# Attention, a top-2 router and eight experts in one kernel: the last group's tail ahead of the first expert, whole-group loads of q and k, and stores from ScalarE's queue

## The chip, the cores and the metric

The kernel runs on one core of a Trainium2 chip. The metric is the device time of one execution in microseconds (us); the time of the kernel before is the median of three runs. The profile is one execution taken with the hardware profiler. Engines are named as in the profile: PE (TensorE matmul) and PEld (its weight load), DVE (VectorE), ACT (ScalarE), POOL (GpSimd), SP (SyncE). L559 is line 559 of the kernel before.

## The reference

Block-causal attention over 8 batches of 8 heads, 576 tokens of 64 elements, and then a mixture of 8 experts over all 4608 tokens; each token goes to two experts.

```python
def _attn_ref(q, k, v):
    scores = scale * np.matmul(q, k.transpose(0, 1, 3, 2))
    mask = block_i >= block_j                      # blocks of 64 positions
    scores = np.where(mask, scores, -1000000000.0)
    attn = softmax(scores)                         # [...] written out with max and sum
    return np.matmul(attn, v)

def _moe_ref(x, w_gate, w_noise, noise, w1, w2):   # x: 4608 x 512, w1: 8 x 512 x 1024, w2: 8 x 1024 x 512
    logits = x @ w_gate
    noise_scale = np.log1p(np.exp(x @ w_noise))
    noisy_logits = logits + noise_scale * noise
    top2 = np.argpartition(-noisy_logits, 2, axis=1)[:, :2]
    # [...] softmax over the two logits gives top2_w
    for e in range(E):
        for k in range(2):
            mask = top2[:, k] == e
            h = np.maximum(x[mask] @ w1[e], 0.0)
            out[mask] += top2_w[mask, k, None] * (h @ w2[e])
    return out
```

## The kernel before

Attention works through four groups (`g`) of two batches, nine tiles of 128 tokens each. A group has 26 slots (`UG`); in each slot a piece of scores is multiplied and exponentiated (`score_unit`), and then everything that was put at that slot runs: transposes of q and k, AV tiles, transposes of x, steps of the router, and loads. AV of a group's second half of heads, its x transposes, its router and its scatters lie in the slots of the next group. The program's order is the order of the code; an engine does its instructions in that order.

```python
def load_qk(g, chunks):
    for ch in chunks:
        for nm, src in (("q", qv), ("k", kv)):
            t = raw_pool.tile([P, 2, 512], BF16, tag="r" + nm)      # raw_pool: bufs=8
            t0 = g * TG + ch
            if ch < 4:
                nc.gpsimd.dma_start(out=t, in_=src[:, t0:t0 + 6:5, :])
            else:
                nc.gpsimd.dma_start(out=t[:, 0, :], in_=src[:, t0, :])
            raws[(g, nm, ch)] = t
```

The router gives each token a row in each of its two experts' tables, and 18 indirect stores a group put the tokens into DRAM (`xd`, one array per half of the tokens). Groups 0 and 1 are half 0, groups 2 and 3 half 1.

```python
def scatter(g, j):
    # [...] one tile of 128 tokens, one of its two experts
    ins = nc.gpsimd.indirect_dma_start(out=xd[half]..., in_=xrs[g][:, idx, :].bitcast(I32), ...)
    tc.add_manual_dep(ins.ins, pace[-1], SYNC_DEP, reason="spreads the descriptors over time")

def load_x(b):                       # the rows of one expert and half, transposed: "row tile"
    half, e = SEQ[b]
    xg = ffn["x"].tile([P, DB, CAP], BF16, tag="xg", name="xg") if b else xa
    ins = nc.sync.dma_start_transpose(out=xg, in_=xd[half][e * CAP:(e + 1) * CAP, 0:Dm])
    # [...] waits for all 36 scatters of the half
```

The experts come in 16 batches (`SEQ`: three experts of half 0, three of half 1, then the halves in turn). A batch has eight steps of layer 1 and five of layer 2; `layer1(b + 1, 0)` stands ahead of `layer2(b, 0)`.

```python
def layer2(b, c):
    yp = av_ps.tile([P, Dm], F32, tag="av")                         # av_ps: bufs=2
    for fb in range(FB):
        nc.tensor.matmul(out=yp, lhsT=hs[b][:, fb, c * P:(c + 1) * P], rhs=w2sb[:, fb, :], ...)
    if e + 1 < E:
        ysb = ffn["y"].tile([P, Dm], BF16, tag="ysb", bufs=4)
        ins = nc.scalar.activation(out=ysb, in_=yp, func=AF.Copy, scale=w)
        pace.append(ins.ins.name)
        nc.sync.dma_start(out=yd[half][e * CAP + c * P:e * CAP + (c + 1) * P, :], in_=ysb)
    if c < LT[e]:
        # yo = yp * w + the gathered row of the token's other expert; scattered to the output by GpSimd

# the last group (g == 3), r0 = 104:
avs, xts_ = (0, 0, 1, 1, 2, 2, 3, 3, 4, 4), range(2, 7)             # slots of AV tiles and x transposes
rsl = (6, 6, 7, 8, 8, 9, 9, 10, 12, 13, 13, 13, 14, 14, 14, 14)     # slots of the 16 router steps
r1 = 14                                                             # slot of the first scatter
# [...]
slot = NG * UG                                                      # 104
for i in range(2):                                                  # slots 104 and 105 stand alone
    run(slot)
    slot += 1
# [...] then one step of the experts, and what was put at the slot, in turn
```

The weighted rows of every expert but the last go to `yd` by a store from SyncE's queue; the row tiles are loaded on the same queue. GpSimd issues all loads of q, k, v and weights, all scatters, gathers and output stores.

Of the kernel before, what the change touches and what calls it, by code (L numbers as in the profile page):

```python
# [19 lines left out]
def kernel(  # L20
# [88 lines left out]
    hq_pool = right.enter_context(tc.tile_pool(name="hq", bufs=1, side="right"))  # L109
    raw_pool = raws_up.enter_context(tc.tile_pool(name="raw", bufs=8, side="right"))  # L110

# [81 lines left out]
    def load_qk(g, chunks):  # L193

        for ch in chunks:
            for nm, src in (("q", qv), ("k", kv)):
                t = raw_pool.tile([P, 2, 512], BF16, tag="r" + nm)
                t0 = g * TG + ch
                if ch < 4:
                    nc.gpsimd.dma_start(out=t, in_=src[:, t0:t0 + 6:5, :])  # L200
                else:
                    nc.gpsimd.dma_start(out=t[:, 0, :], in_=src[:, t0, :])
                raws[(g, nm, ch)] = t

# [25 lines left out]
    def transpose_qk(g, nm, ch):  # L230
        dst = qT if nm == "q" else kT
        tp = tr_ps.tile([P, 1024], BF16, tag="tr")


        if ch in (0, 1, 2, 3):
            raw = raws[(g, nm, ch)]
            p0, p1, c0, nb = 0, P, ch * 1024, 16
        else:
            raw = raws[(g, nm, 4)]
            p0 = 0 if ch == "4A" else 64  # L240
            p1, c0, nb = p0 + 64, 4 * 1024, 8
        n = nb * 64
        if nm == "q":
            to = tp[:, 0:n].rearrange("p (b r j) -> p b r j", b=nb, r=8)
        else:
            to = tp[:, 0:n].rearrange("p (r b j) -> p b r j", b=nb, r=8)
        for r in range(8):
            if nb == 16:
                for hf in range(2):
                    nc.tensor.transpose(to[64 * hf:64 * hf + 64, :, r, :], raw[:, hf, r * 64:(r + 1) * 64], ident)  # L250
            else:
                nc.tensor.transpose(to[p0:p1, :, r, :], raw[p0:p1, 0, r * 64:(r + 1) * 64],  # L252
                                    ident[p0:p1, p0:p1])
        if nm == "q":
            nc.vector.tensor_copy(dst[p0:p1, c0:c0 + n], tp[p0:p1, 0:n])
        else:
            ko = dst[p0:p1, c0:c0 + n].rearrange("p (b j r) -> p b j r", b=nb, j=8)
            ki = tp[p0:p1, 0:n].rearrange("p (r b j) -> p b j r", r=8, b=nb)
            if ch == 1:
                nc.vector.tensor_copy(ko, ki)  # L260
            else:
                nc.scalar.activation(out=ko, in_=ki, func=AF.Copy)  # L262
        if ch == 0:

            nc.vector.tensor_copy(dst[64:128, 72 * 64:73 * 64], dst[64:128, 0:64])
# [104 lines left out]
    def router(g):  # L370
# [37 lines left out]

        c2 = rt.tile([P, TG, E], F32, tag="c2")
        nc.vector.tensor_tensor_scan(out=c2.rearrange("p t e -> p (t e)"),  # L410
# [32 lines left out]
        yield  # L443
        ps = rt.tile([P, E, TG], F32, tag="ps")
        nc.vector.tensor_tensor(out=pos, in0=pos, in1=ms, op=ALU.mult)
        nc.vector.tensor_tensor(out=ps, in0=pos[:, 1], in1=pos[:, 0], op=ALU.subtract)
        yield
        sl2 = rt.tile([P, 2, TG], F32, tag="sl2")
        pk = rt.tile([P, 2, E, TG], F32, tag="pk")
        nc.vector.tensor_tensor(out=pk, in0=oh, in1=ps.unsqueeze(1).to_broadcast([P, 2, E, TG]),  # L450
# [30 lines left out]
    def scatter(g, j):  # L481
        half = g // 2
        idx, i = divmod(j, 2)
        ins = nc.gpsimd.indirect_dma_start(  # L484
            out=xd[half].bitcast(I32), out_offset=bass.IndirectOffsetOnAxis(
                ap=slots[:, g * TG + idx, i:i + 1], axis=0),
            in_=xrs[g][:, idx, :].bitcast(I32), in_offset=None,
            bounds_check=XR - 1, oob_is_err=False)
        tc.add_manual_dep(ins.ins, pace[-1], SYNC_DEP, reason="spreads the descriptors over time")
        key = f"scat{half}"  # L490
        if scat[half]:
            tc.declare_no_dep(ins.ins, group=key, reason="rows of one half are distinct")
        tc.add_to_no_dep_group(key, ins.ins)
        scat[half].append(ins.ins.name)
# [14 lines left out]
    def load_rec(half):  # L509
        rc = rec_pool.tile([P, E, CT, NREC], I32, tag="rc", name="rc")  # L510
        ins = nc.sync.dma_start(out=rc.rearrange("p e c w -> p (e c) w"),
# [6 lines left out]
    def read_rec(half):  # L518
# [3 lines left out]
        def tmp(nm, dt=F32):  # L522
            return rec_pool.tile([P, E, CT], dt, tag=nm, name=nm)


        is0 = tmp("is0")
        nc.vector.tensor_tensor(out=is0, in0=f[0], in1=rowid, op=ALU.is_equal)
        wr = rec_pool.tile([P, E, CT], F32, tag=f"wrow{half}", name="wrow")
        nc.vector.tensor_tensor(out=wr, in0=is0, in1=f[4], op=ALU.mult)
# [6 lines left out]
        nc.vector.tensor_scalar(oth, oth, 0.0, float(XR - 1), op0=ALU.max, op1=ALU.min)  # L536
        orow = rec_pool.tile([P, E, CT], I32, tag=f"orow{half}", name="orow")
        nc.vector.tensor_copy(orow, oth)
# [8 lines left out]
        nc.vector.tensor_tensor(out=mt, in0=mt, in1=fill, op=ALU.mult)  # L547
        tr = rec_pool.tile([P, E, CT], I32, tag=f"trow{half}", name="trow")
        nc.vector.tensor_scalar(tr, mt, -1.0, float(TOKM), op0=ALU.mult, op1=ALU.add)
# [16 lines left out]
    def layer2(b, c):  # L566
# [7 lines left out]
        if e + 1 < E:  # L574
            ysb = ffn["y"].tile([P, Dm], BF16, tag="ysb", bufs=4)
            ins = nc.scalar.activation(out=ysb, in_=yp, func=AF.Copy, scale=w)  # L576
            pace.append(ins.ins.name)
            nc.sync.dma_start(out=yd[half][e * CAP + c * P:e * CAP + (c + 1) * P, :], in_=ysb)
        if c < LT[e]:
# [34 lines left out]
    NB = len(SEQ)  # L614
    rec_pool = keep
    todo = {}
# [47 lines left out]
    def spread_nz(eh, hf):  # L664
# [7 lines left out]
        nc.vector.tensor_copy(dst[:, :, :, 8], src[:, :, :, hf, 8])  # L672

    def flags():
        for i in range(NH):
# [29 lines left out]
    nc.gpsimd.dma_start(out=wgn[:, :, E:2 * E], in_=moe_w_noise.rearrange("(b p) e -> p b e", p=P))  # L705
    load_qk(1, (4, 0, 1))

# [3 lines left out]
    for g in range(NG):  # L711
# [6 lines left out]
        if not last:  # L718
            for nm, ch, i in (("q", 0, 14 if g else 19), ("k", 0, 17 if g else 22), ("q", "4B", 22), ("k", "4B", 21)):
                at(s0 + i, transpose_qk, g + 1, nm, ch)  # L720
            for i, (fn, *a) in enumerate(v_loads(g + 1)):
                at(s0 + 9 + i, fn, *a)
            at(s0 + 13, load_qk, g + 1, (2,))
            at(s0 + 16, load_qk, g + 1, (3,))
        if g + 2 < NG:
            for i, ch in ((20, 4), (22, 0), (24, 1)):
                at(s0 + i, load_qk, g + 2, (ch,))
        for i, a in enumerate((15, 16, 17, 18, 18, 19, 20, 21, 22, 23)):
# [11 lines left out]
        else:  # L740
            avs, xts_ = (0, 0, 1, 1, 2, 2, 3, 3, 4, 4), range(2, 7)
            rsl = (6, 6, 7, 8, 8, 9, 9, 10, 12, 13, 13, 13, 14, 14, 14, 14)
            r1 = 14
# [19 lines left out]
    for k in range(4):  # L763
        at(2 * UG - 6 + k, load_w, wE, 0, k)
        at(2 * UG + 20 + k, load_w, wE, 1, k)
    for u in range(NG * UG):
        score_unit(*divmod(u, UG))
        run(u)
        if u == 3 * UG + 13:
            raws_up.close()  # L770
            ffn["x"] = raws_up.enter_context(tc.tile_pool(name="xgp", bufs=3, side="right", reuse_waits="tile"))
            wM = raws_up.enter_context(tc.tile_pool(name="wM", bufs=1, side="right", reuse_waits="tile"))
            at(3 * UG + 19, load_x, 0)
            at(3 * UG + 20, load_x, 1)
            at(3 * UG + 21, load_rec, 0)
            at(4 * UG, load_x, 2)
            for k in range(4):
                at(3 * UG + 22 + 3 * k, load_w, wM, 2, k)

    slot = NG * UG  # L780
    at(slot + 6, read_rec, 0)
    at(slot + 80, flags)
    at(slot + 90, read_flags)
    steps = []
    for b in range(NB):
# [3 lines left out]
        steps += [(layer2, b, c) for c in range(CT)]  # L789
    for i in range(2):  # L790
        run(slot)
        slot += 1
    WL = {}
    XL = {(2, 3): 3, (3, 1): 4, (3, 5): 5, (4, 2): 6}
    for b in range(5, NB - 2):
        XL[b, 1] = b + 2
    for fn, b, j in steps:
        fn(b, j)
        if fn is layer1:
            if (b, j) == (2, 3):  # L800
                load_rec(1)
            if (b, j) in XL:
                load_x(XL[b, j])
            if (b, j) == (3, 3):
                read_rec(1)
# [9 lines left out]
        slot += 1  # L815
        if slot == NG * UG + 6:
            top.close()
            wL = top.enter_context(tc.tile_pool(name="wL", bufs=2, reuse_waits="tile"))
            ffn["y"] = top.enter_context(tc.tile_pool(name="yp", bufs=4, reuse_waits="tile"))
            ffn["yg"] = [ffn["y"].tile([P, Dm], BF16, name=f"yg{i}", bufs=1) for i in range(GB)]  # L820
            for t in ffn["yg"]:
                nc.vector.memset(t, 0.0)
            for i, pool in enumerate((wL, wL, wE, wE, wM)):
                for k in range(4):
                    WL[3 + 2 * i + k // 2, (2, 6)[k % 2]] = (pool, 3 + i, k)
    assert not todo, sorted(todo)
# [89 lines left out]
```

## Time and profile before

| | |
|---|---|
| time, median of 3 runs | 493.08 us (488.45 to 499.44) |
| span of the profiled execution | 504.7 us |
| PE busy | 409.2 us (81%) |
| ACT busy | 253.2 us (50%) |
| POOL busy | 255.8 us (51%) |
| DVE busy | 161.2 us (32%) |
| layer 1, 960 matmuls of `hp` from `xg` | 137.7 us, 305 ns each |
| layer 2, 640 matmuls of `yp` | 143.8 us, 382 ns each |
| scatters, 72 on GpSimd | 71.2 us, 988 ns each |
| stores of `yd`, 70 on SP's queue | 128 KB each, landing 2.2 us after the issue (median) |
| row tile loads of `xg`, 15 on SP's queue | landing after 9.0 us (median) |
| loads of two tiles of q, 16 on GpSimd | 256 KB each, landing after 8.1 us (median) |

The profile's page gives busy times by engine, the span in 40 slices, the chain of waits that ended last, and groups of instructions by line. A group's line reads: line, engine, operation, output and input tiles, shape, count, busy us and mean ns, and the idle time of the engine just ahead, with what ended it. The attention part ends near 145 us; the experts begin with the first row tile, `xa`.

### The profile page before, as it was taken

Reading aid. Unit: us, or ns where it says so; the run is one execution under the profiler, and the core shown is the slowest. Engines: PE = TensorE matmul, PEld = TensorE weight load, DVE = VectorE, ACT = ScalarE, POOL = GpSimd, SP = SyncE. Lnnn points to the kernel's source line nnn. Section 1 sums busy time; section 2 is a strip of 40 time slices with the busy share of each in tenths; the row PEclk is TensorE's granted clock in tenths of the full one; section 3 lists DMA queues with packets and bytes.
Section 4 is the critical chain, followed back from the end, with each engine's and each line's share of the span. In section 5 each row is a group of like instructions: output and inputs, shape, how many; then the busy total and the mean of one; then the engine's idle time right before and its main releaser. Section 6 shows DMA issues by size and latency. Waiting matters only on the chain.

```text
span 504.7 us, 9922 instructions
## 1 busy us (share of the span) xinstructions
PE 409.2 (81%) x3952; PEld 250.9 (50%) x3952; DVE 161.2 (32%) x508; ACT 253.2 (50%) x343; POOL 255.8 (51%) x309
## 2 busy tenths in 40 slices
PE   2889889889730999919599999999942999999980
PEld 2466656557420746504346655664521565556540
DVE  1677687787840580003000011011100102211220
ACT  2989888878820245513335544554502454455210
POOL 8776674588577456723002234337240546656530
PEclk9989989989875999978989999999985999999995
DMA  8999999899929983462926877997999789994320
GB/s 136 158 147 186 214 185 206 202 126 166 206 107 183 190 192 111 163 102 76 201 75 135 173 169 172 190 165 134 136 104 183 184 178 221 200 202 138 123 79 17
DMA packets 134826, 78.68 MB, mean 156 GB/s; under 512 B 96193, under 2 KB 124611, under 8 KB 134772
## 3 DMA queue, kind: packets, MB, share of 16 engines
q0 software_dynamic: 70560, 55.79, 68.7%
q1 hardware_dynamic: 64212, 22.18, 24.5%
q8 instruction: 33, 0.54, 0.4%
q14 instruction: 21, 0.17, 0.1%
HBM read 68.28 MB, written 33.13 MB: 201 GB/s over the span
## 4 chain that ended last, share of the span: by engine, by line
PE 53%; DMA 17%; issue 9%; DVE 8%; ACT 6%; POOL 5%; SPq 0%; POOLq 0%; DVEq 0%; ACTq 0%
PE yp L571 21%; PE hp L559 18%; DMA yd<-ysb 5%; DMA xg<-xd 4%; ACT esc L295 4%; PE sc L292 3%; PE av L334 3%; PE tp L250 2%; POOL out_dram L583 2%; DMA xa<-xd 2%; DMA yg<-yd,orow 2%; DVE xr L350 2%; DMA xd<-xr,slots 2%; PE av L345 2%; DMA t<-in_q_dram 2%
## 5 line engine op out<-in xcount | busy, mean ns | idle before, releaser
L559 PE MATMUL hp<-xg,w1sb 128*128 128x320 bf16 x960 | 137.7, 305 | 32.6 <-ACT hq L562 16.4
L559 PEld LDWEIGHTS <-w1sb 128*128 128x128 bf16 x1024 | 101.5, 100 | 94.8 <-DMA xa<-xd 18.1
L571 PE MATMUL yp<-w2sb,hq 128*128 128x512 bf16 x640 | 143.8, 382 | 1.2 <-DVE yo L581 1.0
L562 ACT ACTIVATE hq<-hp 128x640 bf16<-128x640 f32 x128 | 90.0, 704 | 105.7 <-PE hp L559 105.6
L581 DVE SCALAR_TENSOR_TENSOR yo<-yp,wrow,yg 128x512 f32<-128x512 f32 x46 | 34.5, 751 | 263.7 <-ACT ysb L576 220.5
L571 PEld LDWEIGHTS <-hq 128*128 128x128 bf16 x640 | 63.0, 98 | 77.0 <-issue 7.2
L295 ACT ACTIVATE esc<-sc 128x1024 bf16<-128x1024 f32 x96 | 94.2, 1026 | 11.5 <-PE sc L292 10.9
L576 ACT ACTIVATE ysb<-yp,wrow 128x512 bf16<-128x512 f32 x70 | 48.1, 687 | 95.1 <-PE yp L571 74.6
L484 POOL DMA_INDIRECT xd<-xr,slots x72 | 71.2, 988 | 47.4 <-issue 12.5
L599 POOL DMA_INDIRECT yg<-yd,orow x46 | 47.6, 1034 | 89.9 <-ACT hq L562 59.7
L583 POOL DMA_INDIRECT out_dram<-yo,trow x46 | 45.8, 995 | 75.4 <-DVE yo L581 62.8
L292 PE MATMUL sc<-hq 64*128 64x512 bf16 (+4 forms) x320 | 40.0, 319 | 11.9 <-ACT esc L295 10.5
L207 POOL DMA_DIRECT2D vt<-in_v_dram x40 | 34.3, 866 | 8.2 <-PE av L345 3.9
L334 PE MATMUL av<-vt,esc 128*128 128x65 bf16 x640 | 32.6, 204 | 5.6 <-DVE xr L350 5.3
L334 PEld LDWEIGHTS <-esc 128*128 128x128 bf16 x640 | 25.7, 104 | 19.3 <-DVE xr L350 11.8
L350 DVE TENSOR_TENSOR xr<-av,rden 128x256 bf16<-128x256 f32 x72 | 30.6, 425 | 2.7
L250 PE MATMUL tp<-ident,t 128*64 128x128 bf16 x512 | 23.1, 239 | 3.4 <-DMA t<-in_q_dram 2.4
L559 PE MATMUL hp<-xa,w1sb 128*128 128x320 bf16 x64 | 10.9, 320 | 18.0 <-DMA xa<-xd 18.0
L262 ACT ACTIVATE hq<-tp 128x1024 bf16<-128x1024 bf16 (+1 forms) x20 | 17.1, 855 | 12.0 <-PE tp L252 6.8
L349 DVE RECIPROCAL rden<-av 128x4 f32<-128x4 f32 x72 | 13.4, 187 | 30.3 <-PE av L334 24.8
L292 PEld LDWEIGHTS <-hq 64*128 64x128 bf16 x320 | 12.6, 96 | 20.2 <-issue 12.6
L250 PEld LDWEIGHTS <-t 128*64 128x64 bf16 x512 | 17.7, 120 | 7.8 <-DMA t<-in_q_dram 2.5
(122 smaller groups left out, 239.2 us busy)
## 6 DMA issues: line engine op xcount, KB each, us to landing
yd<-ysb SPq DMA_DIRECT2D x70, 128.0 KB, 2.2
w1sb<-in_moe_w_dram POOLq DMA_DIRECT2D x16, 512.0 KB, 7.1
w2sb<-in_moe_w_dram POOLq DMA_DIRECT2D x16, 512.0 KB, 6.5
t<-in_q_dram POOLq DMA_DIRECT2D x16, 256.0 KB, 8.1
t<-in_k_dram POOLq DMA_DIRECT2D x16, 256.0 KB, 8.0
vt<-in_v_dram POOLq DMA_DIRECT2D x32, 128.0 KB, 8.4
xd<-zero SPq DMA_DIRECT2D x16, 132.0 KB, 7.3
xd<-xr,slots POOLq DMA_INDIRECT x72, 4.1
```

What stands on the lines that cost most here:

```text
L250: nc.tensor.transpose(to[64 * hf:64 * hf + 64, :, r, :], raw[:, hf, r * 64:(r + 1) * 64], ident)
L292: nc.tensor.matmul(out=sc[:, hf, off:off + z - a], lhsT=kT[sl, c0 + jt * P:c0 + jt * P + P], rhs=qT[sl, c0 + a:c0 + z], start=True, stop=True)
L295: ins = nc.scalar.activation(out=esc[:, hh, :, piece * 512:(piece + 1) * 512], in_=sc, func=AF.Exp, scale=scale)
L334: nc.tensor.matmul(out=av[:, hh, :], lhsT=esc[:, hh, hf, c:c + P], rhs=vb[:, 4 * hf + jt, h, :], start=(jt == 0), stop=(jt == ib))
L350: nc.vector.tensor_tensor(out=xr[:, idx, st * SET * D:(st + 1) * SET * D].rearrange("p (h d) -> p h d", h=SET), in0=av[:, :, 0:D], in1=rde ...
L484: ins = nc.gpsimd.indirect_dma_start(out=xd[half].bitcast(I32), out_offset=bass.IndirectOffsetOnAxis(ap=slots[:, g * TG + idx, i:i + 1], a ...
L559: nc.tensor.matmul(out=hp[:, n, 0:NW], lhsT=w1sb[:, db, fb * P:(fb + 1) * P], rhs=xgs[b][:, db, n * NW:(n + 1) * NW], start=(db == 0), sto ...
L562: ins = nc.scalar.activation(out=hs[b][:, fb, :].rearrange("p (n w) -> p n w", n=2), in_=hp[:, :, 0:NW], func=AF.Relu)
L571: nc.tensor.matmul(out=yp, lhsT=hs[b][:, fb, c * P:(c + 1) * P], rhs=w2sb[:, fb, :], start=(fb == 0), stop=(fb == FB - 1))
L576: ins = nc.scalar.activation(out=ysb, in_=yp, func=AF.Copy, scale=w)
L583: ins = nc.gpsimd.indirect_dma_start(out=out, out_offset=bass.IndirectOffsetOnAxis(ap=trow[half][:, e, c:c + 1], axis=0), in_=yo, in_offse ...
L599: ins = nc.gpsimd.indirect_dma_start(out=yg, out_offset=None, in_=yd[half][0:e * CAP, :], in_offset=bass.IndirectOffsetOnAxis(ap=orows[hal ...
```

## The change

It has several parts. The last group's AV, its transposes and the first three router steps run in seven slots ahead of the first expert step, to lie in the wait for the first row tile. q and k of groups 1 to 3 come in one load each, to spare GpSimd's issues; two buffers hold whole groups. The weighted rows are stored from ScalarE's queue, so that SyncE's queue holds row tiles alone. Scatters are paced by the activation before the last; the records (`rc`) and their working tiles move into the space of the raw q and k; the loads of weights for experts 1 and 2 and of row tiles are put at other slots, and the clearing of the gather tiles is spread out.

```diff
-    raw_pool = raws_up.enter_context(tc.tile_pool(name="raw", bufs=8, side="right"))
+    raw_pool = raws_up.enter_context(tc.tile_pool(name="raw", bufs=2, side="right"))
[...] load_qk writes slices of one tile per group (group 0 alone uses it)
+    def load_all(g, nm):
+        raws[(g, nm)] = raw_pool.tile([P, TG, 512], BF16, tag="r" + nm, name="raw")
+        nc.gpsimd.dma_start(out=raws[(g, nm)], in_=(qv if nm == "q" else kv)[:, g * TG:(g + 1) * TG, :])
[...]
-        tc.add_manual_dep(ins.ins, pace[-1], SYNC_DEP, reason="spreads the descriptors over time")
+        tc.add_manual_dep(ins.ins, pace[-2], SYNC_DEP, reason="spreads the descriptors over time")
[...]
-            nc.sync.dma_start(out=yd[half][e * CAP + c * P:e * CAP + (c + 1) * P, :], in_=ysb)
+            nc.scalar.dma_start(out=yd[half][e * CAP + c * P:e * CAP + (c + 1) * P, :], in_=ysb)
[...]
-    load_qk(1, (4, 0, 1))
+    load_all(1, "q")
+    load_all(1, "k")
[...]
-            at(s0 + 13, load_qk, g + 1, (2,))
-            at(s0 + 16, load_qk, g + 1, (3,))
         if g + 2 < NG:
-            for i, ch in ((20, 4), (22, 0), (24, 1)):
-                at(s0 + i, load_qk, g + 2, (ch,))
+            at(s0 + 14, load_all, g + 2, "q")
+            at(s0 + 17, load_all, g + 2, "k")
[...]
-            avs, xts_ = (0, 0, 1, 1, 2, 2, 3, 3, 4, 4), range(2, 7)
-            rsl = (6, 6, 7, 8, 8, 9, 9, 10, 12, 13, 13, 13, 14, 14, 14, 14)
+            avs, xts_ = (0, 0, 1, 1, 2, 2, 3, 3, 4, 4), (2, 3, 4, 5, 5)
+            rsl = (5, 6, 6, 7, 7, 8, 8, 9, 10, 10, 11, 11, 12, 12, 13, 13)
             r1 = 14
[...]
-        at(2 * UG + 20 + k, load_w, wE, 1, k)
+        at(3 * UG + 2 + 4 * k, load_w, wE, 1, k)
[...]
-            at(3 * UG + 19, load_x, 0)
+            at(3 * UG + 18, load_x, 0)
+            at(3 * UG + 19, load_rec, 0)
             at(3 * UG + 20, load_x, 1)
-            at(3 * UG + 21, load_rec, 0)
-            at(4 * UG, load_x, 2)
+            at(3 * UG + 21, load_x, 2)
             for k in range(4):
-                at(3 * UG + 22 + 3 * k, load_w, wM, 2, k)
+                at(4 * UG + 3 + 4 * k, load_w, wM, 2, k)
[...]
-    at(slot + 6, read_rec, 0)
+    at(slot + 14, read_rec, 0)
+    for i in range(GB):
+        at(slot + 15 + i, clear_yg, i)
[...]
-    for i in range(2):
+    for i in range(7):
         run(slot)
         slot += 1
-    XL = {(2, 3): 3, (3, 1): 4, (3, 5): 5, (4, 2): 6}
-    for b in range(5, NB - 2):
+        open_top(slot)
+    XL = {(2, 1): 3, (2, 2): 4}
+    for b in range(3, NB - 2):
         XL[b, 1] = b + 2
[...]
-            if (b, j) == (2, 3):
-                load_rec(1)
             if (b, j) in XL:
                 load_x(XL[b, j])
+            if (b, j) == (2, 1):
+                load_rec(1)
```

## The prediction

> **What bounds the kernel now.** I read the page's slices first, then the waits, then the chain and the timeline around each long wait. The profiled execution has a span of 504.7 us, while the median without a profile is 493.08 (488.45 to 499.44), so sizes are read in the profile and differences are taken off about 490.
>
> The slices of the page (a digit is a busy share in tenths):
>
> ```profile
> PE   2889889889730999919599999999942999999980
> POOL 8776674588577456723002234337240546656530
> DMA  8999999899929983462926877997999789994320
> ```
>
> The waits (total, times, longest, in us):
>
> ```profile
> ACT ysb L576 <- DMA yd<-ysb: 19.5, 2, 18.2
> PE hp L559 <- DMA xa<-xd: 18.0, 1, 18.0
> PE hp L559 <- ACT hq L562: 16.4, 1, 16.4
> PE hp L559 <- DMA xg<-xd: 16.2, 2, 10.8
> ```
>
> The busy times by stretch (stretch, length, PE, weight loads, VectorE, ScalarE, GpSimd, clock, DMA share, GB/s):
>
> ```profile
> 145.00:164.00 19.00, 0.99 (x12) 0.55 (x8) 0.86 (x3) 0.00 (x0) 13.97 (x17) 0.53 0.76 157
> 164.00:191.00 27.00, 25.90 (x266) 17.07 (x265) 18.93 (x67) 9.83 (x18) 12.61 (x14) 0.95 1.02 184
> ```
>
> The timeline around each long wait (start, duration; in brackets the idle time ahead and what ended it):
>
> ```profile
> 150.88 0.98 POOL L484 DMA_INDIRECT xd<-xr,slots  x1 [0.30 <-issue]
> 153.62 4.66 SPq L504 DMA_TRANSPOSE xa<-xd  x1
> 163.25 1.73 PEld L559 LDWEIGHTS <-w1sb 128*128 128x128 bf16 x8 [18.13 <-DMA xa<-xd]
> ...
> 218.29 6.16 SPq L504 DMA_TRANSPOSE xg<-xd  x1
> 226.67 2.31 PE L559 MATMUL hp<-xg,w1sb 128*128 128x320 bf16 x8 [10.78 <-DMA xg<-xd]
> 251.96 2.31 PE L559 MATMUL hp<-xg,w1sb 128*128 128x320 bf16 x8 [5.44 <-DMA xg<-xd]
> ...
> 352.74 15.95 SPq L504 DMA_TRANSPOSE xg<-xd  x1
> 368.78 18.42 SPq L578 DMA_DIRECT2D yd<-ysb  x5
> 387.50 8.77 PE L559 MATMUL hp<-xg,w1sb 128*128 128x320 bf16 x48 [16.38 <-ACT hq L562]
> ```
>
> Each slice is 504.7/40 = 12.6 us. PE is at eight tenths or more nearly everywhere; the drops are four single waits, and the waits view gives their sizes: 18.0 us for the first row tile `xa`, 10.8 and 5.4 us for two later row tiles `xg`, 16.4 us in the batch near 369 us. They sum to 50.6 us, and the rest is PE work that the change doesn't touch. In the stretch 145 to 164 PE is busy 0.99 of 19 us while GpSimd is busy 13.97: the row tile waits for group 1's last scatter (issued 150.88), and GpSimd issues scatters one after another, 0.97 + 0.30 = 1.27 us each. Right behind the wait, 164 to 191 is a batch that took 27.6 us (163.26 to 190.9) where the later ones take 17.37 (263.30 to 280.67): the last group's AV, transposes and router sit inside it.
>
> **What the Trainium skill says.** (1) "DMA: Bandwidth & Descriptors", section "Issuing engines are not separate DMA queues": transfers from ScalarE, SyncE and GpSimd run on the same 16 engines, and another issuer saves only sequencer time. (2) Same page, "Queues, rings and completion order": SyncE and ScalarE each own a row of rings, and an engine goes round the rows packet by packet. The trace agrees with the picture of one ring now: the first store after the slow transpose landed 17.28 us after its issue at 368.78, against a median of 2.2. (3) "Perfetto Trace Analysis", section "DMA Instruction — HWDGE (DVE, Sync)": the descriptor generator is locked by one issuer at a time, and the wait for it is inside the profiled window. No run here shows it, for ScalarE issues no transfer before the change. (4) "TensorE: Matmul & The Clock Gate", section "What's actually happening": after an idle window of some 3.4 us PE restarts at half its clock. The trace agrees: eight layer-1 matmuls take 2.31 us behind each wait, 1.09 in a run.
>
> **Part 1, the tail of the last group.** Seven slots instead of two run before the first layer 1, so all of group 3's second AV half, its transposes and its logits come first in PE's order; in the changed program's order 32 layer-1 matmuls then stand before the two prefix-sum matmuls. Moved out of the first batch: 27.6 − 17.4 = 10.2 us. The moved work fits: PE work of some 8 us (AV 0.87 + 1.01 + 1.65, transposes 3.1, logits 1.4), VectorE 6 tiles x 0.6 + 3.1 us of copies; it ends near 153 and lies in the wait. About −10, if `xa` comes no later.
>
> **Part 2, GpSimd's queue ahead of `xa`.** Groups 1 to 3 issue 2 loads in place of 10: 24 fewer at 0.73 us = 17.5 us of GpSimd time. Little of this is near the scatters. Between 79.18 (first scatter) and 150.88 there are 36 scatters x 1.28 = 46 us, ten v loads 9, four q/k loads 3, four weight loads 3: 61 of 72 us, the rest waits, among them 10.6 us for an exp (pace). The four q/k loads go, and pacing on the activation before the last takes off a few us. Against it: group 3's q and k are asked for at slots 40 and 43, so 1.05 MB more goes ahead of expert 0's weights, whose landing frees the issue slots that scatters 4 to 7 wait for: at about 0.2 MB/us some 5 us there. Net: last scatter of group 1 near 145, landing +2.5, transpose +9.6 (as 153.62 to 163.26): `xa` near 158, −5. The wait falls from 18 to about 5 us.
>
> **Part 3, group 3's scatters.** Before, they run from 190.80 (router done at 189.8) to 215.22, and 218.29 to 226.67 is the transpose. After, the router's second part ends about 10 us behind `xa`, near 168, and no longer decides; GpSimd does: group 2's 18 scatters and 3 weight loads end near 171, group 3's 18 plus a load and a gather 25 us later, 196; +2.5 + 8.4 + about 1: the row tile of batch 3 is there near 208. PE has done batches 0 and 1 and the first layer of 2 by 158 + 19 + 17.4 + 8.7 = 203. So a wait of about 5 us is left, and layer 1 of batch 3 starts at 208 against 226.67: −19 with parts 1 and 2 included.
>
> **Part 4, the next tile.** Its load is issued right behind the third instead of behind stores that end at 240.15. It lands near 216 and is needed near 226. The 5.4 us wait and its cold start (2.31 − 1.09 = 1.2) go: −6.5. Sum so far −25.
>
> **Part 5, stores on ScalarE.** 70 issues leave SyncE (0.32 us each there) and go into ScalarE's order. In a layer-2 step of 1.73 us ScalarE works 0.69, so 0.32 + about 0.1 fits. The 16.4 us jam can't recur in its old form, since no store stands behind a transpose in its queue. I credit it little: 504.7 − 16.4 is 488, close to the fastest run, so the median run has at most a part of it. But SyncE's transposes no longer wait behind stores, and start when the buffer is free: at layer 2's start, the very time of the stores. Their issue took 2.4 to 6.8 us in the steady part; a store held by the generator stops ScalarE, then PE after two `yp` buffers. I charge 0.5 us x 12 batches = +6.
>
> **Part 6, the first group.** q and k of group 1 arrive whole: 1.18 MB each at about 0.2 MB/us (early slices 200 GB/s) is 5.9 us each from 25 on, k near 38 to 40, while the first k transpose stands at 36.8: +2 in the attention part, mostly swallowed by the wait for `xa`, +1.
>
> Sum from about 489 (no jam): −25 + 6 + 1 = 471; rounded with a little left for the jam's part in the median: **470 us**.
>
> **The rivals.** (a) *Transfers are the bound.* For it: the DMA row is 9 in most slices to 139 us and again from 353, 198 GB/s with PE 72 of 72 us busy. Then earlier starts only queue earlier; the gain stops at part 1, about 480. Against: in slice 11 (139 to 151) DMA is at 2 and GpSimd issues without pause, and in 191 to 216 its share is 0.40. (b) *ScalarE's queue becomes the new wait*: each transpose issue of 5 us holds a store, costing 2 to 3 us x 12 batches = 24 to 36: about 490 to 500. For it: the overlap is now systematic. Against: issues of 2.4 to 5 us start 1.1 + 1.73 + 0.69 = 3.5 us ahead of the first store. (c) *The jam was in most runs*: then its 16 us come on top and the time is 455.
>
> **Range and chances.** The scatters' end moves by ±4, the store charge between 0 and 15, the jam between 0 and −12: 454 to 486 for 8 in 10. Faster by over 2% is under 483.2. I give 0.82 to faster, 0.13 to within 2%, 0.05 to slower.
>
> **What would show it.** AV, transposes and logits between 144 and 153 with `xa` still to come; wait for `xa` about 5 us; first batch about 19 us; first scatter of group 3 near 171, not behind the router; one wait for `xg` of about 5 us near 203 and none after it; stores on ScalarE's queue of 0.3 us, some longer beside a transpose. Wrong would be: `xa` landing at 163 or later, a load wait of over 5 us near 36 to 44, or ScalarE's stores of several us in most batches with PE gaps behind them.

## The result, and the profile after

The changed kernel takes 476.62 us (median of four runs, 475.57 to 477.86); the kernel before, on the same chip, 493.98 (488.45 to 499.44). The ratio is 0.9686, 95% interval 0.9598 to 0.9773. Some executions of any kernel are disturbed and some per cent longer; they are left out of all comparisons below, but four profiles are of such a run (before, stores_sp, stores_sp_2 and all_three), so what those four show of waits need not be in every run. The profile after is of the run of 475.57 us; its span is 473.8.

The slices of the page after (11.8 us each):

```profile
PE   3886988989988959499999999999899998999980
POOL 8763073458877775363301243444454573666430
DMA  9999999989888999838996786987969998934320
```

Counting from 0: the holes of before at 11 and 12 (ahead of the experts), at 17 and at 29 and 30 are gone; a dip to 6 has come at slice 3 (36 to 47 us), and one to 5 and 4 at slices 14 and 16 (166 to 201). The waits of the kernel after (total, times, longest):

```profile
ACT ysb L581 <- DMA yd<-ysb: 10.3, 2, 7.6
POOL xd L489 <- DMA w2sb<-in_moe_w_dram: 8.8, 1, 8.8
PE hp L564 <- ACT hq L567: 7.6, 2, 6.3
PE hp L564 <- DMA xg<-xd: 5.1, 1, 5.1
PE tp L257 <- DMA raw<-in_k_dram: 3.9, 1, 3.9
```

PE no longer waits for `xa`; 50.6 us of long PE waits have become 16.6. But the busy times by stretch (the columns of the prediction) show that the work didn't move up by the difference:

```profile
36.00:50.00 14.00, 9.36 (x132) 6.01 (x129) 4.51 (x14) 7.04 (x10) 4.14 (x5) 0.59 1.85 182
145.00:164.00 19.00, 16.55 (x304) 12.96 (x304) 15.03 (x52) 6.92 (x11) 14.62 (x18) 0.84 0.92 168
164.00:191.00 27.00, 20.97 (x118) 11.82 (x117) 12.97 (x51) 9.28 (x15) 16.61 (x18) 0.87 1.24 177
224.00:430.00 206.00, 202.62 (x1200) 118.40 (x1211) 29.47 (x55) 105.22 (x152) 89.38 (x93) 1.00 0.87 184
```

The idle 18 us of 145 to 164 are filled, with PE busy 16.55 against 0.99. The stretch behind them, which was full before (25.90 of 27), has holes now (20.97). From 224 to 430 PE is busy 202.62 of 206; in the profile of before it was 180.55. And 36 to 50 has lost work: PE ran at a granted clock of 0.59 there.

The timeline after, at the long waits of PE:

```profile
40.21 0.64 PE L257 MATMUL tp<-ident,raw 64*64 64x64 bf16 x8 [3.88 <-DMA raw<-in_k_dram]
...
162.76 4.51 PE L564 MATMUL hp<-xa,w1sb 128*128 128x320 bf16 x32
177.71 2.29 PE L564 MATMUL hp<-xg,w1sb 128*128 128x320 bf16 x8 [5.14 <-DMA xg<-xd]
180.22 9.42 PE L576 MATMUL yp<-w2sb,hq 128*128 128x512 bf16 x39 [0.22 <-issue]
198.13 8.76 PE L564 MATMUL hp<-xg,w1sb 128*128 128x320 bf16 x48 [6.32 <-ACT hq L567]
...
215.36 8.86 PE L564 MATMUL hp<-xg,w1sb 128*128 128x320 bf16 x64
```

The first layer 1 starts at 162.76, half a microsecond earlier than before (163.26), now without a wait. Then the second row tile is late by 5.14 us, and in batch 1 a wait of 6.32 stands behind ScalarE. The last eight of the 64 matmuls at 215.36 are the first layer 1 of batch 3; it starts near 223.1 (215.36 + 7/8 x 8.86), against 226.67 before, and that of batch 4 near 240.4 against 251.96.

The chain of waits after (start, length, what) says what held batch 1:

```profile
157.81 19.76 DMA xg<-xd
177.57 0.14 issue
177.71 2.29 PE hp L564 x8
180.00 0.22 issue
180.22 2.53 PE yp L576 x7
182.75 0.02 issue
182.77 0.70 ACT ysb L581
183.47 0.02 issue
183.49 12.71 DMA yd<-ysb
```

The second row tile took 19.76 us from issue to landing; then one store of 128 KB took 12.71, and ScalarE, which has four buffers for these rows, waited for it with layer 1's results behind. The stores' issue is short (0.33 us each), but their median landing is 5.1 us where it was 2.2.

**Where the time went.** When PE loads the first weights of the last score unit of each half group (us, from the timelines); "a half group ends" below means this point:

| half group | 1 | 2 | 3 | 4 | 5 | 6 | 7 | 8 |
|---|---|---|---|---|---|---|---|---|
| before | 25.3 | 40.7 | 57.3 | 73.9 | 91.6 | 108.1 | 125.6 | 141.2 |
| after | 24.1 | 46.2 | 64.7 | 82.4 | 101.3 | 116.7 | 134.5 | 150.6 |

In this pair of profiles the attention part has become 9.4 us longer, which begins at the wait at 40. So three theories were to be tested. (T1) Group 1's whole load of k costs the attention its 9 us, and with it the change loses them. (T2) The gain is that of the tail. The rival is that the tail only fills one wait and is given back in the next, and that stores on ScalarE's queue made the gain. (T3) What bounds the start of the experts is GpSimd's scatters of group 3, held by weight loads among them.

### The profile page after: what moved, and what is told of

Read it like the earlier page. It is cut to its first block, busy times and chain, and to the rows that moved or that the text cites. A ratio compares the mean times of both kernels' runs of the same rounds, so it can differ in the third digit from the quotient of the medians.

```text
span 473.8 us, 9816 instructions
## 1 busy us (share of the span) xinstructions
PE 414.4 (87%) x3936; PEld 256.0 (54%) x3952; DVE 162.2 (34%) x508; ACT 253.9 (54%) x343; POOL 241.8 (51%) x285
## 3 DMA queue, kind: packets, MB, share of 16 engines
q1 hardware_dynamic: 54132, 13.00, 17.4%
## 4 chain that ended last, share of the span: by engine, by line
PE 55%; DMA 17%; POOL 9%; issue 9%; DVE 4%; ACT 3%; POOLq 0%; ACTq 0%; SPq 0%; DVEq 0%
PE hp L564 23%; PE yp L576 19%; DMA yd<-ysb 4%; DMA xg<-xd 4%; DMA raw<-in_k_dram 3%; PE av L339 3%; PE sc L297 3%; POOL out_dram L588 2%; PE tp L254 2%; DMA vt<-in_v_dram 2%; DMA xd<-xr,slots 2%; POOL xd L489 2%; ACT esc L300 2%; PE av L350 2%; POOL vt L210 1%
## 5 line engine op out<-in xcount | busy, mean ns | idle before, releaser
L564 PE MATMUL hp<-xg,w1sb 128*128 128x320 bf16 x960 | 136.4, 303 | 12.8 <-ACT hq L567 7.6
L576 PE MATMUL yp<-w2sb,hq 128*128 128x512 bf16 x624 | 139.9, 381 | 2.4 <-DVE yo L586 1.4
L300 ACT ACTIVATE esc<-sc 128x1024 bf16<-128x1024 f32 x96 | 94.7, 1026 | 16.6 <-PE sc L297 15.9
L297 PE MATMUL sc<-hq 64*128 64x512 bf16 (+4 forms) x320 | 43.5, 343 | 12.0 <-ACT esc L300 10.9
L339 PE MATMUL av<-vt,esc 128*128 128x65 bf16 x640 | 35.2, 213 | 4.1 <-DVE xr L355 3.9
L339 PEld LDWEIGHTS <-esc 128*128 128x128 bf16 x640 | 28.0, 110 | 19.1 <-DVE xr L355 9.2
L254 PE MATMUL tp<-ident,raw 128*64 128x128 bf16 x512 | 25.2, 254 | 2.9 <-DMA raw<-in_q_dram 2.3
L254 PEld LDWEIGHTS <-raw 128*64 128x64 bf16 x512 | 19.5, 130 | 7.7 <-issue 3.1
L260 DVE COPY hq<-tp 128x1024 bf16<-128x1024 bf16 (+1 forms) x24 | 14.7, 612 | 9.4 <-PE tp L254 6.8
## 6 DMA issues: line engine op xcount, KB each, us to landing
w2sb<-in_moe_w_dram POOLq DMA_DIRECT2D x16, 512.0 KB, 19.3
```

Of the source, the lines that this page charges most:

```text
L297: nc.tensor.matmul(out=sc[:, hf, off:off + z - a], lhsT=kT[sl, c0 + jt * P:c0 + jt * P + P], rhs=qT[sl, c0 + a:c0 + z], start=True, stop=True)
L300: ins = nc.scalar.activation(out=esc[:, hh, :, piece * 512:(piece + 1) * 512], in_=sc, func=AF.Exp, scale=scale)
L339: nc.tensor.matmul(out=av[:, hh, :], lhsT=esc[:, hh, hf, c:c + P], rhs=vb[:, 4 * hf + jt, h, :], start=(jt == 0), stop=(jt == ib))
L564: nc.tensor.matmul(out=hp[:, n, 0:NW], lhsT=w1sb[:, db, fb * P:(fb + 1) * P], rhs=xgs[b][:, db, n * NW:(n + 1) * NW], start=(db == 0), sto ...
```

## The experiments

The first four ran on a chip on which the kernel before takes 508.5 to 515.3 us. All four kernels there show a PE clock of 0.5 to 0.7 in three or more slices between 100 and 195 us, and waits which the profile puts to "remote" and "issue" on several engines at once; what causes them stays open. So I read their timelines up to 100 us, and their times only against each other. The next eight ran on two other chips, each beside a control.

**g1_chunks.** Group 1's q and k in tile pairs, as before:

```diff
-    load_all(1, "q")
-    load_all(1, "k")
+    load_qk(1, (4, 0, 1))
[...]
+        if g == 0:
+            at(s0 + 13, load_qk, 1, (2,))
+            at(s0 + 16, load_qk, 1, (3,))
```

> The changed kernel, with group 1's q and k alone loaded in tile pairs again, at their old places. Theory: the attention part is some 9 us longer in the changed kernel because k of group 1 arrives as one piece (wait of 3.9 us at 40 us) and because PE then runs in half-clock windows. Then here no load wait above 1 us stands between 33 and 45 us, PEclk is back near 1.0 between 36 and 50 us, the last score unit is multiplied near 142 to 145 us instead of 151.2, the first scatter is issued near 79 to 81 instead of 87.8, and the time is 467 to 472. Rival 1: the lost time has another cause (the throttle, other groups' whole loads, the later pacing): the last score unit stays at 149 or later, time 474 to 478. Rival 2: the attention part gets shorter but the end of the scatters doesn't, and the time gained turns into a wait for xa: last unit near 143, wait for xa of 6 us or more, time 474 to 477.

Its stretch from 36 to 50 (busy times by stretch), and below it the same of tail_back, which keeps the whole loads, on the same chip:

```profile
36.00:50.00 14.00, 13.10 (x287) 9.60 (x283) 10.50 (x31) 13.17 (x16) 7.68 (x11) 1.00 1.71 186
```

```profile
36.00:50.00 14.00, 9.91 (x147) 6.53 (x144) 5.08 (x16) 7.78 (x10) 4.25 (x6) 0.66 1.85 183
```

The k transpose starts at 36.38 with no wait, the clock is 1.00 in place of 0.66, and PE does 287 matmuls in place of 147. The half groups end at 40.2, 58.9 and 74.7 against 45.8, 63.8 and 80.6 in tail_back, and the first scatter is issued at 80.25 and not at 85.80. The cause of the longer attention up to there is thereby shown: 5 to 6 us come from group 1's loads, of which some 3.7 are the later k transpose itself (40.05 in tail_back) and some 2 come behind it, where the clock is lower. On the two other chips the attention part ends at 142.1 (all_three) and 142.7 (w1_early) with all loads in pairs, and at 147.9 and 148.4 in their controls: 5.8 and 5.7 us, and not the 9.4 of the first pair of profiles. The last unit came at 162.2 and the time at 493.5 and 494.4, outside of what was expected, on this chip. No run of the changed kernel stood beside it; tail_back and stores_sp there took 503.1 to 509.7.

**all_chunks.** As g1_chunks, and groups 2 and 3 in pairs at their old slots.

> The changed kernel, with q and k of groups 1, 2 and 3 all loaded in tile pairs at their old slots (the tail, the stores from ScalarE and the other moves are kept). Theory: group 1's whole load does the harm and those of groups 2 and 3 are neutral: within 2 us of the kernel with group 1's alone in pairs, 467 to 473. Rival 1: the 24 issues of GpSimd saved by whole loads matter for the scatters: last scatter of half 0 some 5 us later than with group 1's pairs alone, and the time 3 to 6 us longer than there. Rival 2: the whole loads of groups 2 and 3 cost as well: 2 to 5 us shorter than there.

491.9 and 498.5 us, with g1_chunks' two runs between them. Half groups 3 to 5 end at 56.5, 72.2 and 90.6, some 2 to 6 us ahead of g1_chunks (58.9, 74.7, 96.2): by this one pair of profiles the other groups' whole loads cost a little too. The other chips don't show it, since there group 1 alone would account for the 5.7 and 5.8 us. The last scatter of half 0 is issued at 150.96, against 151.56: the issues that GpSimd saves with whole loads bring no earlier end of the scatters. Rival 2 has this timeline for it, but not the time.

**stores_sp** and **stores_sp_2.** The stores from SyncE again:

```diff
-            nc.scalar.dma_start(out=yd[half]..., in_=ysb)
+            nc.sync.dma_start(out=yd[half]..., in_=ysb)
```

> The changed kernel, with the stores of the weighted rows issued from SyncE again. Theory: the stores on ScalarE gain by themselves only that no store stands behind a transpose of xg; the wait of 6.3 us at 192 us (ScalarE waiting for a slow store) stays or grows here, and a jam of some 16 us behind a slow transpose can come back: 477 to 490, with a PE wait for hq of over 10 us where a transpose takes over 12 us to issue. Rival 1: the queue is neutral: 475 to 478. Rival 2: ScalarE's queue costs (slower landing of the stores, 5.1 us against 2.2): 468 to 472 here, and landing is back near 2 us.

504.3 and 509.7 us, ratio to before 0.9898 (0.9769 to 1.0027): it looked as though the queue were worth much. So it was run again beside a control:

> The changed kernel with the stores from SyncE again, beside its control. Theory, as the first run of it (0.990 of the kernel before) makes likely: ScalarE's queue is worth 8 to 16 us by itself, since stores stand behind transposes on SyncE and ScalarE's four buffers run out: PE waits of over 4 us for hq behind a store in at least two batches, time 8 to 16 us over the control. Rival: the first run was long by its chip alone, and the queue is worth less than 4 us where the jam near 370 us doesn't come.

471.3 to 472.8 us against 465.7 and 469.6 of the control; as ratios to before 0.9623 (0.9499 to 0.9747) and 0.9616 (0.9452 to 0.9780). The theory falls: where nothing jams, the queue is worth little, up to 4 us and perhaps nothing. The profile, however, of an execution of 485.2 us, has this in the timeline of PE:

```profile
373.50 9.47 PE L564 MATMUL hp<-xg,w1sb 128*128 128x320 bf16 x48 [3.98 <-ACT hq L567]
399.75 8.31 PE L564 MATMUL hp<-xg,w1sb 128*128 128x320 bf16 x48 [5.89 <-ACT hq L567]
421.24 6.68 PE L564 MATMUL hp<-xg,w1sb 128*128 128x320 bf16 x48 [2.28 <-ACT hq L567]
```

Its waits name the cause (ScalarE for a store's buffer):

```profile
ACT ysb L581 <- DMA yd<-ysb: 19.1, 4, 7.7
```

Behind 300 us PE waits 12.2 us for ScalarE here, 17.2 in stores_sp (1.8, 11.2 and 4.3) and 16.4 in before: in all three profiles with stores on SyncE. In the eleven profiles with stores on ScalarE the longest such wait there is 3.4 us. How often the jam comes isn't measured. From the first matmul of batch 3 to the end of the profile the eleven with stores on ScalarE take 248.0 to 254.6 us, the three with stores on SyncE 267.7 to 278.0; but these three executions took 485.2, 506.6 and 518.7 us, none of the shorter ones was profiled, and so the queue is not shown to be the cause.

**tail_back** and **tail_back_2.** The last group's tail at its old slots:

```diff
-            avs, xts_ = (0, 0, 1, 1, 2, 2, 3, 3, 4, 4), (2, 3, 4, 5, 5)
-            rsl = (5, 6, 6, 7, 7, 8, 8, 9, 10, 10, 11, 11, 12, 12, 13, 13)
+            avs, xts_ = (0, 0, 1, 1, 2, 2, 3, 3, 4, 4), range(2, 7)
+            rsl = (6, 6, 7, 8, 8, 9, 9, 10, 12, 13, 13, 13, 14, 14, 14, 14)
[...]
-    at(slot + 14, read_rec, 0)
+    at(slot + 6, read_rec, 0)
[...]
-    for i in range(7):
+    for i in range(2):
```

> The changed kernel, with the last group's AV, transposes and router steps at their old slots again (two slots ahead of the first layer 1), all else kept. Theory: in the changed kernel the moved work lay wholly in the time in which xa was still to come, so here the first layer 1 waits for xa until about 162 and the moved work lies behind it: first batch some 10 us longer, time 484 to 488. Rival: the later waits of the changed kernel (5.1 us for the second row tile, 6.3 us for a store) take up what the tail gives, since both end at times set by transfers: those waits shrink here by 8 us or more and the time is 476 to 480.

503.1 to 504.6 us, 0.9831 (0.9749 to 0.9914) of before; without a control it could not be sized. Again, with one:

> The changed kernel with the last group's tail at its old slots, beside its control. Theory: what lies ahead of the first layer 1 is mostly free, for the first row tile lands only near 160; put back it adds 7 to 10 us to the first batch, and since group 3's router and scatters come later too, the end is 6 to 10 us later than the control. Rival: the waits behind it (second row tile, store) take it up and the end is within 3 us of the control.

476.4 to 480.1 us (median 478.5) against 465.7 and 469.6: the tail is worth some 11 us. But not in the way in which I had thought. The timeline of tail_back_2, and below it that of control_2:

```profile
162.75 2.31 PE L564 MATMUL hp<-xa,w1sb 128*128 128x320 bf16 x8 [11.48 <-DMA xa<-xd]
...
224.83 2.31 PE L564 MATMUL hp<-xg,w1sb 128*128 128x320 bf16 x8 [10.37 <-DMA xg<-xd]
```

```profile
174.52 2.29 PE L564 MATMUL hp<-xg,w1sb 128*128 128x320 bf16 x8 [3.78 <-DMA xg<-xd]
...
216.01 1.26 PE L564 MATMUL hp<-xg,w1sb 128*128 128x320 bf16 x8 [0.77 <-ACT hq L567]
```

Its first batch ends at 189.3, that of control_2 at 185.5: only 4 us are gained in the batch itself, for in control_2 PE waits for the second row tile (3.78 us, then matmuls from a cold start). Batch 3 starts at 224.8 against 216.0, which is 8.8 of the 11 us. The first scatter of group 3 waits in tail_back_2, where it is issued at 190.18 and in control_2 at 181.08:

```profile
190.18 1.00 POOL L489 DMA_INDIRECT xd<-xr,slots  x1 [7.08 <-ACT ysb L581]
```

It waits for the router, which ends at 189.4 (170.9 in control_2), and for the activation that paces it, which ends at 190.2; the two are not separated here. The last scatter is issued at 215.42 and 207.15. So the earlier tail brings the scatters forward, and these set batch 3.

**control** and **control_2.** The changed kernel as it is.

> The changed kernel unaltered, to have it on the chip of the runs beside it. The first measurement gave 0.9686 of the kernel before; 0.960 to 0.977 again here. The k wait of 3.9 us at 36 to 40 us, the waits of 5 us for the second row tile and of 6 us behind a store near 190 us are expected again, within 2 us each.

466.6 to 472.6 us on its chip, 0.9584 (0.9424 to 0.9744) of before. The waits were there again, with other sizes: 2.9 us for k, 1.8 for the second row tile, 5.3 behind a store, and 4.6 for `xa`, which had not been there in the first profile.

> The changed kernel unaltered, for the two part-undone kernels beside it, which so far ran on a chip where all four kernels stalled at 100 to 190 us. 0.955 to 0.975 of the kernel before.

465.7 and 469.6 us, 0.9616 of before.

**w2_late.** The w2 loads of expert 2 behind group 3's scatters:

```diff
-                at(4 * UG + 3 + 4 * k, load_w, wM, 2, k)
+                at(4 * UG + (3, 7, 26, 28)[k], load_w, wM, 2, k)
```

It rests on GpSimd's timeline of the kernel after:

```profile
176.69 0.79 POOL L230 DMA_DIRECT2D w2sb<-in_moe_w_dram  x1 [1.14 <-DMA xd<-xr,slots]
177.79 0.99 POOL L489 DMA_INDIRECT xd<-xr,slots  x1 [0.31 <-issue]
179.09 0.98 POOL L489 DMA_INDIRECT xd<-xr,slots  x1 [0.30 <-issue]
180.37 0.97 POOL L489 DMA_INDIRECT xd<-xr,slots  x1 [0.30 <-issue]
181.35 0.81 POOL L230 DMA_DIRECT2D w2sb<-in_moe_w_dram  x1
182.46 1.00 POOL L489 DMA_INDIRECT xd<-xr,slots  x1 [0.30 <-issue]
183.76 0.97 POOL L489 DMA_INDIRECT xd<-xr,slots  x1 [0.30 <-ACT ysb L581]
185.46 0.97 POOL L489 DMA_INDIRECT xd<-xr,slots  x1 [0.73 <-ACT ysb L581]
195.23 0.97 POOL L489 DMA_INDIRECT xd<-xr,slots  x1 [8.80 <-DMA w2sb<-in_moe_w_dram]
```

Count from the load at 176.69: the scatter that waits for its landing is the eighth issue behind it. It need not have anything to do with the load's data.

> The changed kernel, with the two w2 loads of expert 2 issued behind group 3's scatters and not between them. Theory: group 3's scatters end at 214 us and not at 196 as predicted because these loads stand among them: GpSimd waits 8.8 us for one of them to land and issues them for 0.8 us each. Then here that wait is gone, the last scatter is issued 8 to 12 us earlier (202 to 206 if batches start as in the changed kernel), and the third half-1 tile's transpose with it. The time moves by less than 6 us, for PE reaches that tile at the same time as before unless the slow store near 190 us is quicker too: 470 to 477. Rival: another lane wait takes its place, the scatters end within 3 us of the control, time the same.

The last scatter is issued at 205.73, in the control at 210.83: 5 us of the expected 8 to 12. Batch 3 waits 4.74 us for its tile all the same and starts at 218.8; the time is 468.2 to 472.5, as the control. With the loads gone, two waits of 2.4 and 2.6 us for earlier scatters and two of 1.2 remained. The theory is not shown by this run, for its own control has no wait for a w2 load among group 3's scatters, but one for a scatter:

```profile
193.40 0.97 POOL L489 DMA_INDIRECT xd<-xr,slots  x1 [6.27 <-DMA xd<-xr,slots]
```

And front_waits, with the w2 loads in place, comes to 205.09. The wait of 8.8 us is thus one of the first profile. What the late loads cost is seen at the tile: its transpose is issued 6.7 us behind the last scatter, in the control 4.2.

**front_waits.** The second row tile ahead of the records, and eight buffers for the stores:

```diff
-            ysb = ffn["y"].tile([P, Dm], BF16, tag="ysb", bufs=4)
+            ysb = ffn["y"].tile([P, Dm], BF16, tag="ysb", bufs=8)
[...]
-            at(3 * UG + 19, load_rec, 0)
-            at(3 * UG + 20, load_x, 1)
+            at(3 * UG + 20, load_rec, 0)
+            at(3 * UG + 19, load_x, 1)
```

> The changed kernel, with the second row tile's transpose issued ahead of the records' load, and eight buffers instead of four for the weighted rows. Theory: the 5.1 us wait for the second row tile and the 6.3 us wait behind a store both go or fall below 2 us, but the end hardly moves: in the changed kernel PE reaches batch 3 at 223.1, just when its row tile lands (issued 217.9, shortest landing 4.7), so the time saved turns into a wait for that tile of 6 to 11 us near 212 to 223: time within 3 us of the control. Rival: the tile also comes earlier with PE, since GpSimd's gather between the scatters waits for PE's progress: 6 to 11 us less than the control.

464.8 to 466.4 us against 466.6 to 472.6 (medians 465.0 and 472.4), 0.9469 (0.9301 to 0.9638) of before. The two waits go, as expected (the two edits are not taken apart), and the end moves: the rival holds in kind. Its size is open, since the interval overlaps with the control's, a fourth execution took 472.4, and the control has one of 466.6. In the timeline batch 3 still waits for its tile, but earlier (control: start near 220):

```profile
214.74 2.31 PE L564 MATMUL hp<-xg,w1sb 128*128 128x320 bf16 x8 [3.26 <-DMA xg<-xd]
```

The last scatter came at 205.09 (control 210.83) though nothing on GpSimd was changed. Its gather among the scatters is paced by PE's batches, and it was issued at 194.75 in place of 200.46.

**all_three.** Both edits together, with all q and k in pairs.

> The changed kernel with q and k of groups 1 to 3 in tile pairs again, with w2 of expert 2 behind group 3's scatters, and with the second row tile ahead of the records and eight buffers for the weighted rows. Theory: the waits hide one another, and only taken away together do they show: attention some 6 to 9 us shorter, the scatters' end 12 to 18 us earlier, no wait over 3 us from the first layer 1 to batch 4; time 458 to 466 where the control has 476 (0.93 to 0.95 of the kernel before). Rival: the first row tile becomes the bound again (a wait of 8 us or more for xa), and no more than 3 to 6 us are gained on the control.

462.3 to 467.2 us (median 464.9), 0.9443 (0.9264 to 0.9621) of before: as front_waits alone. The profile is of an execution of 479.6 us, so its later waits need not be those of the 462 to 467. The half groups end like those of before (40.7, 57.3, 74.0, 91.8, 108.4, 125.8, 142.1), the first layer 1 starts at 157.49 in place of 164.85, and batch 1 begins 10 us earlier than in the control (177.35 against 187.29). Then PE waits 5.8, 6.2 and 7.4 us, ahead of batch 2, in layer 2 of batch 1 and ahead of batch 3. The scatters behind the last of these, in GpSimd's timeline:

```profile
165.47 0.77 POOL L230 DMA_DIRECT2D w1sb<-in_moe_w_dram  x1
...
174.27 0.97 POOL L489 DMA_INDIRECT xd<-xr,slots  x1 [0.30 <-issue]
190.69 0.97 POOL L489 DMA_INDIRECT xd<-xr,slots  x1 [15.45 <-DMA w1sb<-in_moe_w_dram]
```

Seven scatters follow the w1 half, and the eighth waits 15.45 us for it. The last scatter is again at 210.83, as in the control, although the attention ended 6 us earlier.

**w1_early.** all_three, with w1 of expert 2 ahead of group 1's last scatters (the line as against the kernel after):

```diff
-                at(4 * UG + (3, 7, 26, 28)[k], load_w, wM, 2, k)
+                at((3 * UG + 14, 3 * UG + 16, 4 * UG + 26, 4 * UG + 28)[k], load_w, wM, 2, k)
```

> The kernel with tile pairs, w2 of expert 2 late, the second row tile first and eight buffers; now w1 of expert 2 is loaded two slots after its pool opens, ahead of group 1's last scatters, and no weight load stands among the scatters of groups 2 and 3. Theory: a GpSimd issue waits until the eighth issue before it has landed (15.5 us behind a w1 half there, 8.8 us behind a w2 half in the changed kernel), so that with no load among the scatters none waits over 4 us, group 3's last scatter is issued at 203 or earlier instead of 211, and the time is 452 to 460, or 0.92 to 0.935 of the kernel before. Rival: the scatters' own landing sets the lanes (transposes in the same engines), the last scatter stays at 207 or later and the time at 462 to 467; or the first row tile is put off by the load by over 4 us and the gain is lost there.

464.1 to 465.1 us and one of 467.1, 0.9484 (0.9390 to 0.9579) of before, beside 465.7 and 469.6 of control_2: not told apart. In the timeline what was expected of the scatters holds: none waits over 3.2 us, and the last is issued at 199.03, against 207.15. But the second rival came true as well:

```profile
162.61 6.91 PE L564 MATMUL hp<-xa,w1sb 128*128 128x320 bf16 x32 [7.61 <-DMA xa<-xd]
```

The w1 halves, issued at 144.06 and 147.74, stand ahead of the last scatters of half 0 (148.83), and the transpose of `xa` is issued 8.0 us behind the last scatter, where it was 4.0 in control_2. The 6 us won in attention are lost in this wait. Batch 3 starts at 212.65 and no lower, for here too the w2 loads stand at the end of the scatters, and the tile's transpose is issued 8.1 us behind the last of them (3.1 in control_2).

## Why the prediction was right, and where its steps failed

The time (476.6 for 470) was inside the range. Yet it is in part luck: a sum of errors that partly cancel. Up to batch 4 the prediction had −25; the profiles show 240.4 − 252.0 = −11.6, of which some −3.6 are there at batch 3 and −8 come from batch 3 to batch 4. Of the −17.4 between the medians, the other 6 fit to the jam's share in the runs of before, which I had credited little; that split is argued, not measured, and the profile of before is of an execution 12.6 us above the median. The runs that undo one part each give as gain some 11 us for the tail, −5 to −6 for the loads of q and k, and 0 to 4 for the stores: 5 to 10 of the 17.4. The pacing, the places of the weight loads and of the row tiles, and with them part 4, were not undone, and their shares stay open.

- **Part 1 (the tail, −10).** The value is right: some 11 us by tail_back_2. The step that failed is "first batch about 19 us": it took 26.7 (162.76 to 189.48), in the profile of before 27.6, for I had no wait for the second row tile in it. The gain came through group 3's scatters instead, as tail_back_2 shows.
- **Part 2 (`xa` near 158, −5).** Worth nothing: the transpose was issued at 153.56, before at 153.62. GpSimd did issue 36 scatters in less time (61.5 us between the first and the last, before 71.7), but they began 8.6 us later, since the attention was late. That the wait for `xa` fell came from PE being late: the tail's last matmuls end near 162.9, and `xa` had landed at 161.6.
- **Part 3 (group 3's scatters, −19 with parts 1 and 2).** The term that was sized worst. The router ended at 172.6 (168 predicted), the first scatter was at 177.79 (171), the last at 213.89 (196), batch 3 at 223.1 (208). The number of loads, four for the scatters of groups 2 and 3, was right, and so was the gather; what was missing is that the queue waits: 8.8 us for a load and 3.5 for PE at the gather. From the first scatter of group 3 to its last it took 36.1 us for the 25 predicted. In the other runs of the changed kernel it is 31.9 (control) and 26.1 (control_2), in front_waits 26.1, in w1_early, with a load ahead of the last one only, 24.0: the 25 hold where the queue doesn't wait, and which wait comes differs from run to run.
- **Part 4 (next tile, −6.5).** Right by the profiles: batch 3 to batch 4 takes 17.3 us instead of 25.3, without a wait. No run undoes it.
- **Part 5 (stores, +6).** The fear behind the charge is not seen: SyncE's transposes took up to 12.8 us to issue, and ScalarE's store issues stayed at 0.33 to 0.48. The Trainium skill's page "Perfetto Trace Analysis", section "DMA Instruction — HWDGE (DVE, Sync)", has a lock that would be in that time; no run here shows it for these two issuers. Seven of the 70 stores of the kernel after begin and end their issue while a transpose is being issued, in 0.33 us each. What came instead is the slower landing (5.1 for 2.2) and one 6.3 us wait on four buffers. Net 0 to −4 by stores_sp_2, and no jam behind 300 us in the profiles with stores from ScalarE.
- **Part 6 (group 1's loads, +1).** Wrong in size. The k tile landed at 40.16 and was wanted at 36.3, as worked out; but PE's clock then stood at half from 39 to 52 us, and the attention part ended 5 to 6 us later for it by g1_chunks, 9.4 in the first pair of profiles. For the kernel after, with its wait of 3.88 us, this fits what the skill's page "TensorE: Matmul & The Clock Gate", section "What's actually happening", says of an idle window of about 3.4 us; I had quoted it for the waits of layer 1 and not applied it to my own new wait. Such a window isn't the whole of it: in control and control_2 the clock was at half from 36 and 34 us on, ahead of the wait for k and behind waits for q of 1.3 and 1.6 us.
- **The rivals.** (a), transfers as the bound, has more in it than I gave: both long waits of PE behind 160 us in the kernel after (5.1 and 6.3) end on a transfer. (b) did not come. (c) would have made it 455.

The versions beyond the change: front_waits, a few lines more, has 465.0 against the control's 472.4 on one chip, with the reserve named there. Putting the attention right (all_three, w1_early) gains some 6 us in the attention part and nothing clear at the end, where the loads of expert 2 stand before one transposed row tile or another (`xa` in w1_early, that of batch 3 in w2_late and w1_early).

## What to carry to other kernels

Work moved into a wait is worth what the next deadline gives back: follow it to the next two transfers (here the second row tile, then the scatters of the last group), not to the end of the stretch. Look at what stands among a chain of small transfers in one engine's order, since a large load there can hold a later issue that has nothing to do with its data. Joining loads into one saves issues but lets the first piece arrive with the last; here PE's wait for it came with a lower clock, and the two together cost 5 to 6 us where 1 was charged.

## What the runs showed of the hardware

- On GpSimd's queue the eighth issue behind a load waited for this load: 8.8 us (w2, kernel after) and 15.45 us (w1, all_three). A trace names the load as the releaser of a scatter that doesn't read it. In all fourteen profiles there are 39 waits of over 2 us that the profile puts to an earlier load of q, k or weights from GpSimd, for a GpSimd issue, and each of the 39 is one of the eighth issue behind that load.
- A w2 half of 0.5 MB lands 6.5 us after its issue in the median of before (5.9 to 15.1, the nine that the trace resolves); in after the one that it resolves took 19.3. A w1 half that went with row tile transposes and scatters took some 25 (165.47 to 190.7 in all_three).
- Stores from ScalarE issue in 0.33 us while SyncE issues a transpose, which takes 2.5 to 12.8 us (kernel after).
- In the nine profiles with group 1's k in one load PE's granted clock is 0.50 from 44 to 48 us, behind waits for k of 2.1 to 3.9 us; in the five with pairs it is 1.00.
- The same kernel before takes 488 to 499 us on one chip and 508 to 515 on another.
